# Moving the Strassen products of one half ahead of its plain output products, in an attention kernel fused with a ReGLU feed-forward

## The chip, the cores and the metric

The kernel runs on one core of one Trainium2 chip. The metric is the device time of one execution in microseconds (us). TensorE (PE) does the matmuls and loads their weights (PEld); VectorE (DVE), ScalarE (ACT) and GpSimd (POOL) work element by element; DMAs are issued from the queues of SyncE (SP), POOL and ACT. Each engine works through its own instructions in program order.

## The reference

Attention over 4 batches, 8 heads, 768 positions and 64 dimensions, with a mask (8 global positions and the last 96) and a distance bias per head; its output, 3072 tokens x 512, goes through a gated feed-forward layer with 1536 hidden columns.

```python
scores = scale * np.matmul(q, k.transpose(0, 1, 3, 2))
...
scores = scores + bias[None, :, :, :]
scores = np.where(keep, scores, -1000000000.0)
...
a = np.exp(scores)
a = a / (np.sum(a, axis=-1, keepdims=True) + 1e-09)
return np.matmul(a, v).astype(np.float32)
...
x = np.ascontiguousarray(attn_out.transpose(0, 2, 1, 3)).reshape(B * S, H * D)
gate = np.maximum(x @ w_gate, 0.0)
val = x @ w_val
return (gate * val @ w_out).astype(np.float32)
```

## The kernel before

**Halves.** The work is cut into 8 halves: half s is batch s // 2 and 384 of its positions. In the text "half 2" is s = 2, the third one (the diff's title counts from one: its "second half" is s = 1 and its "third half" s = 2). Attention runs one half ahead of the feed-forward layer, so while the feed-forward work of one half fills TensorE, the next half's attention is placed between.

**Attention of a half** (`attention_pieces`) goes by four pairs of heads, p = 0 to 3. `piece_qk` issues the scores of a pair (L397, 8 matmuls in an even half, 10 in an odd one) into four banks of the PSUM pool `x`, then ScalarE's exps (L406, tile `es`) and VectorE's masks (L359). `piece_av` (the P·V product, L427) takes one bank of `x` for each head; ScalarE takes the logarithm of the row sums (L436, `lnd`) and, after the second head, the exp that gives the inverse (L441, `rcp`). `piece_norm` (L446, "norm p") multiplies on VectorE into chunk p of `xT`, the feed-forward input, one multiply for each head; each frees one bank of `x`. The pool `x` has five banks, used in turn: an allocation waits for the release of the one five allocations earlier.

**Keys and queries of a half** (`early_pieces`) come through ks and qs (DMA), eight casts on GpSimd (L363, into `kqc`), three DMA transposes on SyncE's queue (L368, into `kqT`), and four reorderings (`piece_order`, "order p", L259 to L265, three copies on GpSimd each) into `kT`, the keys in the order that the scores read.

**Feed-forward of a half** (`ffn_pieces(c)`) has two lists. f1: for each of 12 column groups fc a `gate` product (4 matmuls, L518; ScalarE's relu L525) and a `val` product (4 matmuls, L518; VectorE multiplies into `ht`, L531). f2: the output product, of three tiles of 128 tokens. A *plain* tile is 12 matmuls of 512 columns in four parts of three (L538), a copy by ScalarE (L543, tile `osb`) and a store on SyncE's queue (L544). From the second half on, tiles 0 and 1 are instead computed by seven Strassen-like products `p4 p3 p1 p2 p5 p6 p7`, six matmuls of 256 columns each (L581):

- p4, p3 and p1 go to banks of the pool `ff` named d, c and a, and ScalarE copies them into two `osb` tiles (L597, L601, L605).
- p2 and p5 each take one bank of the pool `x`, and VectorE adds and subtracts them (L609, L610; L614, L615).
- p6 goes on adding to bank c; VectorE adds it (L622) and the tile is stored from SyncE's queue (L623). p7 does the same with bank a (L627, L628). Both stores run through `store` (L591).

The products read sums of `ht` (`sum_de`, `sum_cb`, `sum_ad`, L574, L565, L569) and five sums of wo, computed once in ten steps on VectorE (`wo_sum`, L804, tiles `bs`). The pool `ff` has three banks, used in turn, the `osb` pool three buffers, used in turn.

The next half begins with `begin` (L546): gate and value matmuls of column group 0 over the first three chunks of `xT` (6 matmuls); the fourth chunk's matmuls come behind the first scores of the half after it.

**The order** on every engine is the order in which `weave` (L659) calls the pieces. It walks through a list of feed-forward pieces with given weights (mostly 0.65, sums 0), and after each it issues those placed items whose position, as a share of the list's total, has been reached. `spread` (L654) gives a list of items evenly spaced positions between two shares.

**The stage of the change** (L821) runs the last four column groups of half 0 and half 1, then f2 of half 0 (three plain tiles, 12 parts) and f2 of half 1 (one plain tile with two sums between, then the products). Its total weight is 25.35. Into it are placed two reorderings of half 2 on ScalarE, the attention of half 2, the early pieces of half 3 and the ten `wo_sum` steps. The stages behind it (L827) each hold one half's f1 and f2, the attention of the next half, and the early pieces of the one after.

Of the kernel before, what the change touches and what calls it, by code (L numbers as in the profile page):

```python
# [15 lines left out]
def kernel(  # L16
# [124 lines left out]
    def fill_ones(eng, i, j):  # L141
        eng.memset(vbuf[i][:, j, :].bitcast(mybir.dt.uint32).rearrange(
            "p (h z) -> p h z", z=D // 2)[:, 0 : 2 * H + 1 : 2, :], 0x3F803F80)
# [217 lines left out]
    def piece_cast(s, p, i):  # L361
        of = (ks_of, qs_of)[i]
        nc.gpsimd.tensor_copy(  # L363
            kqc[:, :, i].rearrange("t n (h d) -> t h n d", d=D)[:, 2 * p : 2 * p + 2],
            of[s][:, 2 * p : 2 * p + 2, :].rearrange("t e (n d) -> t e n d", n=NN))

    def piece_x(s, n):
        nc.sync.dma_start_transpose(  # L368
            out=kqT[s % 2].rearrange("d i p t -> d (i p) t")[:, :, n * 128 : (n + 1) * 128],
            in_=kqc[:, n].rearrange("t i z -> t (i z)"))  # L370

    def piece_order(s, p):
        b, half = divmod(s, 2)
        copy = nc.scalar.copy if s == 2 and p >= 2 else nc.gpsimd.tensor_copy
        put_keys(copy, copy, kT[b % 2][p], kNb[s % 2][:, p], half)

    def early_pieces(s):
        out = [(0.0, lambda p=p, i=i: piece_cast(s, p, i)) for i in range(2) for p in range(HP)]
        out += [(0.0, lambda n=n: piece_x(s, n)) for n in range(NN)]
        out += [(0.0, lambda p=p: piece_order(s, p)) for p in range(HP)]  # L380
        return out
# [26 lines left out]
    def piece_qk(s, p, g):  # L408
        if g == 0:
            pair_scores(s, p)  # L410
        if g < 2:
            pair_exps(s, p, g)
        if g > 0:
            masks(s, p, g - 1, steps_later)

    def piece_av(s, p, e):
        b, half = divmod(s, 2)
        h = 2 * p + e
        vb = vbuf[b % 2]
        av = psum["x"].tile([128, 512], FP32, name="x_ps")  # L420
        av_of[s, p, e] = av
        av3 = av[:, 0:QH].rearrange("d (n p) -> d n p", n=NN)
        todo = [by[half, j] for g in steps_later[half] for j in g]
        for i, (j, a, w, m) in enumerate(todo):
            es, c = es_of[s, p, j]
            z0 = 2 * D * h + (D if e == 0 else 0)
            nc.tensor.matmul(av3[:, :, a : a + w],  # L427
                             lhsT=vb[:, j, z0 : z0 + 128],
                             rhs=es[:, e, c : c + NN * w].rearrange("k (n p) -> k n p", n=NN),
                             start=(i == 0), stop=(i == len(todo) - 1),  # L430
                             skip_group_check=True)
        o0, d0 = (0, 64) if e == 0 else (64, 0)
        if e == 0:
            av_of[s, p, "l"] = rc_pool.tile([128, QH], FP32, name="lnd")
        ln = av_of[s, p, "l"]
        nc.scalar.activation(ln[o0 : o0 + 64], av[d0 : d0 + 64, 0:QH], AF.Ln, bias=0.0, scale=1.0)  # L436
        if e == 1:
            if s not in xT_of:
                xT_of[s] = xt_pool.tile([128, N_DC, QH], BF16, name="xT")
            rc = av_of[s, p, "r"] = rc_pool.tile([128, QH], FP32, name="rcp")  # L440
            nc.scalar.activation(rc, ln, AF.Exp, bias=0.0, scale=-1.0)  # L441

    def piece_norm(s, p):
        for e in range(2):
            r = slice(64 * e, 64 * e + 64)
            nc.vector.tensor_tensor(xT_of[s][r, p, :], av_of[s, p, e][r, 0:QH], av_of[s, p, "r"][r],  # L446
                                    op=ALU.mult)
# [45 lines left out]
    def attention_pieces(s):  # L493
        QK = lambda p: [(0.15, lambda g=g: piece_qk(s, p, g)) for g in range(3)]
        AV = lambda p: [(0.29, lambda e=e: piece_av(s, p, e)) for e in range(2)]
        N = lambda p: [(0.0, lambda: piece_norm(s, p))]
        g = QK(3)
        a = AV(2)
        gap = [(0.0, lambda: None)]
        return (QK(0) + QK(1) + AV(0) + N(0) + gap + QK(2) + AV(1) + N(1) + gap  # L500
                + g[0:1] + a[0:1] + g[1:2] + a[1:2] + g[2:3] + N(2) + AV(3) + N(3))
# [152 lines left out]
    def spread(items, first, last):  # L654

        n = len(items)
        return [(first + (i + 0.5) / n * (last - first), f) for i, (_, f) in enumerate(items)]

    def weave(f_items, *placed):  # L659
        total = sum(t for t, _ in f_items)  # L660
        a_items = sorted((x for p in placed for x in p), key=lambda x: x[0])
        done, ai = 0.0, 0
        for t, f in f_items:
            f()
            done += t
            while ai < len(a_items) and a_items[ai][0] * total <= done:
                a_items[ai][1]()
                ai += 1
        for _, f in a_items[ai:]:
            f()  # L670
# [84 lines left out]
    f1_0, f2_0 = ffn_pieces(0)  # L755
    f1_1, f2_1 = ffn_pieces(1)
# [20 lines left out]
    for f in ("m1 g0 m3 v0 m2 g1 K3 K2 m0 g3 K1 S30 S31 g2 K0 S20 v3 S11 v1 S21 A3 N3 v2 S00 S01 "  # L777
              "g5 A2 S10 g4 g6 A0 N2 v5 v4 N0 A1 N1 g7 v7 v6").split():
        i = int(f[1])
# [20 lines left out]
    def wo_sum(name, part):  # L800
        i = slice(part * N_FC // 4, (part + 1) * N_FC // 4)
        x, y = (wo_sb[:, (int(b[1]) - 1) * N_FC // 2 :][:, i, (int(b[2]) - 1) * DM // 2 : int(b[2]) * DM // 2]
                for b in (name[:3], name[4:]))
        nc.vector.tensor_tensor(late["bs"][name][:, i], x, y, op=ALU.add if "+" in name else ALU.subtract)  # L804

    G = [slice(2 * GW * i, 2 * GW * (i + 1)) for i in range(N_FC // GW)]
# [7 lines left out]
    for f in (*casts[:7], lambda: nc.gpsimd.tensor_copy(held, wo_sb[0:1, N_FC - 1, 0:1]),  # L814
# [3 lines left out]
    load_v_half(3)  # L818
    weave(f1_1[G[0]])
    weave(f1_1[G[1]], [(0.1 + 0.12 * j, lambda j=j: fill_ones(nc.vector, 0, j)) for j in range(NT)])  # L820
    weave(f1_0[G[2]] + f1_1[G[2]] + f2_0 + f2_1,  # L821
          [(0.33, order_k[2]), (0.38, order_k[3])],
          spread(attention_pieces(2), 0.375, 0.9), spread(early_pieces(3), 0.58, 0.88),
          spread([(0.0, lambda name=name, part=part: wo_sum(name, part)) for name in late["bs"] for part in range(2)],
                 0.1, 0.74))

    for c in range(2, NHALF):  # L827
        placed = []
# [6 lines left out]
        f1, f2 = ffn_pieces(c)  # L835
# [36 lines left out]
```

## Time and profile before

| | us |
|---|---|
| median of 3 runs (lowest, highest) | 242.32 (241.63, 242.71) |
| profiled execution | 242.01 |
| its span, first to last instruction | 240.2 |
| f1 of half 1 ends, f2 of half 0 begins | about 57 |
| first plain part of half 1 | 67.5 |
| first product | 71.4 |
| first gate matmul of half 2 | 76.6 |
| first scores of half 3 | 78.8 |

The granted TensorE clock is 1.000 over the span. Times in the profile are us from the first instruction. A timeline line gives start, length, engine, line, operation, output and inputs, and a count of merged instructions; behind it, in brackets, the engine's idle time before and what ended it. PE's matmuls overlap: a matmul's duration is longer than the step to the next one's start, so where PE's pace matters, the text goes by starts.

### The profile page before, as it was taken

How to read it: one execution, taken by the hardware profiler on the slowest of the kernel's cores; microseconds unless marked ns; L12 is line 12 of the kernel's file. 1: busy time of each engine (PE TensorE's matmuls, PEld its weight loads, DVE VectorE, ACT ScalarE, POOL GpSimd, SP SyncE). 2: the span in 40 equal slices, each digit the busy share in tenths (PEclk: the TensorE clock that was granted, in tenths of full speed). 3: DMA queues.
4: the chain of work that ended last, by engine and by line, in shares of the span. 5: the costliest groups of instructions: out<-in, count | busy, mean ns of one | idle time of the engine just before them, and what ended most of it. 6: DMA issues, size and time to landing. Idle time of an engine off the chain costs nothing.

```text
span 240.2 us, 5363 instructions
## 1 busy us (share of the span) xinstructions
PE 233.5 (97%) x1945; PEld 146.3 (61%) x1945; DVE 172.5 (72%) x456; ACT 153.6 (64%) x347; POOL 87.0 (36%) x202
## 2 busy tenths in 40 slices
PE   7999999999998999999999999999999999999994
PEld 3655556665457566676568566676658566676663
DVE  6785965769587597866888679766887677764643
ACT  5897873438775777738774777738874677733330
POOL 6767892308414733541539042721414000000000
PEclk9999999999999999999999999999999999999999
DMA  6999999994975995299245966198241200030003
GB/s 197 186 197 178 257 231 220 184 161 80 268 162 128 235 213 97 44 143 289 54 91 71 246 181 114 20 179 265 50 88 44 90 0 0 3 128 4 4 26 105
DMA packets 69603, 31.42 MB, mean 131 GB/s; under 512 B 47160, under 2 KB 66616, under 8 KB 69576
## 3 DMA queue, kind: packets, MB, share of 16 engines
q0 software_dynamic: 31744, 8.71, 35.1%
q1 hardware_dynamic: 36616, 21.45, 34.3%
q10 hardware_dynamic: 1216, 0.92, 1.2%
q8 instruction: 15, 0.25, 0.4%
q14 instruction: 12, 0.10, 0.1%
HBM read 28.41 MB, written 6.29 MB: 144 GB/s over the span
## 4 chain that ended last, share of the span: by engine, by line
PE 91%; ACT 3%; DVE 2%; DMA 1%; issue 1%; ACTq 0%; DVEq 0%
PE ff_ps L518 54%; PE ff_ps L538 9%; PE ff_ps L581 8%; PE x_ps L427 5%; PE x_ps L397 4%; PE x_ps L581 3%; PE t_ps L459 2%; PE s_ps L341 2%; DMA kq<-in_k_dram 1%; PE t_ps L272 1%; ACT lnd L436 1%; PE t_ps L310 1%; DVE xT L446 1%; ACT rcp L441 1%; PE s_ps L321 1%
## 5 line engine op out<-in xcount | busy, mean ns | idle before, releaser
L518 PE MATMUL ff_ps<-xT,wv 128*128 128x384 bf16 x384 | 80.2, 326 | 1.1 <-DVE osb L622 1.0
L518 PE MATMUL ff_ps<-xT,wg 128*128 128x384 bf16 x384 | 80.6, 326 | 0.4 <-ACT grelu L525 0.4
L531 DVE TENSOR_TENSOR ht<-ff_ps,grelu 128x384 bf16<-128x384 f32 x96 | 53.1, 554 | 29.2 <-PE ff_ps L518 16.7
L525 ACT ACTIVATE grelu<-ff_ps 128x384 bf16<-128x384 f32 x96 | 47.3, 492 | 35.9 <-DVE ht L531 17.8
L518 PEld LDWEIGHTS <-wv 128*128 128x128 bf16 x384 | 36.1, 97 | 24.1 <-issue 2.3
L518 PEld LDWEIGHTS <-wg 128*128 128x128 bf16 x384 | 35.9, 98 | 24.1 <-issue 0.9
L406 ACT ACTIVATE es<-x_ps 128x360 bf16<-128x360 f32 (+2 forms) x96 | 36.7, 443 | 20.8 <-PE x_ps L397 20.7
L359 DVE TENSOR_TENSOR es<-es,m_all 128x432 bf16<-128x432 bf16 (+4 forms) x108 | 31.0, 333 | 8.5 <-ACT es L406 8.1
L446 DVE TENSOR_TENSOR xT<-x_ps,rcp 64x384 bf16<-64x384 f32 x48 | 26.6, 555 | 9.7 <-ACT rcp L441 9.0
L436 ACT ACTIVATE lnd<-x_ps 64x384 f32<-64x384 f32 x48 | 23.3, 485 | 12.3 <-PE x_ps L427 11.6
L538 PE MATMUL ff_ps<-wo_sb,ht 128*128 128x512 bf16 x120 | 30.2, 379 | 0.0
L363 POOL CAST kqc<-ks 128x384 bf16<-128x384 f32 x24 | 11.4, 518 | 30.7 <-DMA ks<-in_k_dram 30.5
L137 POOL DMA_DIRECT2D vbuf<-in_v_dram x25 | 21.6, 876 | 2.3 <-DMA wv<-in_moe_w_val_dram 1.8
L427 PE MATMUL x_ps<-es,vbuf 128*128 128x216 bf16 (+4 forms) x216 | 21.5, 225 | 0.0
L427 PEld LDWEIGHTS <-vbuf 128*128 128x128 bf16 x216 | 15.8, 97 | 7.7
L538 PEld LDWEIGHTS <-ht 128*128 128x128 bf16 x120 | 10.8, 97 | 9.4
L363 POOL CAST kqc<-qs 128x384 bf16<-128x384 f32 x24 | 12.2, 548 | 11.9 <-DMA qs<-in_q_dram 11.9
L263 POOL COPY kT<-kqT 128x240 bf16<-128x240 bf16 x16 | 7.1, 441 | 24.5 <-DMA kqT<-kqc 22.4
L441 ACT ACTIVATE rcp<-lnd 128x384 f32<-128x384 f32 x24 | 12.6, 524 | 0.8
L259 POOL COPY kT<-kqT 128x360 bf16<-128x360 bf16 x10 | 5.7, 572 | 19.3 <-DMA kqT<-kqc 19.3
L347 ACT ACTIVATE ef<-s_ps 128x720 bf16<-128x720 f32 (+2 forms) x16 | 11.0, 711 | 1.7 <-PE s_ps L341 1.3
L397 PE MATMUL x_ps<-kqT,kT 64*128 64x216 bf16 (+4 forms) x216 | 11.6, 224 | 0.2
(115 smaller groups left out, 252.1 us busy)
## 6 DMA issues: line engine op xcount, KB each, us to landing
out_dram<-osb SPq DMA_DIRECT2D x22, 256.0 KB, 3.6
ks<-in_k_dram SPq DMA_DIRECT2D x6, 768.0 KB, 7.0
qs<-in_q_dram SPq DMA_DIRECT2D x6, 768.0 KB, 13.9
vbuf<-in_v_dram POOLq DMA_DIRECT2D x21, 120.0 KB, 8.1
wg<-in_moe_w_gate_dram POOLq DMA_DIRECT2D x3, 512.0 KB, 8.8
wv<-in_moe_w_val_dram POOLq DMA_DIRECT2D x3, 512.0 KB, 10.0
wo_sb<-in_moe_w_out_dram POOLq DMA_DIRECT2D x1, 1536.0 KB, 20.3
kq<-in_q_dram ACTq DMA_DIRECT2D x2, 192.0 KB, 4.4
```

The costliest lines, as they stand in the source:

```text
L137: nc.gpsimd.dma_start(out=v_dst(b, NG + r0, NG + r0 + n, j), in_=v[b, :, KT * j + r0 : KT * j + r0 + n, :].rearrange("h p d -> p h d"))
L359: nc.vector.tensor_mul(for_all, for_all, mk)
L363: nc.gpsimd.tensor_copy(kqc[:, :, i].rearrange("t n (h d) -> t h n d", d=D)[:, 2 * p : 2 * p + 2], of[s][:, 2 * p : 2 * p + 2, :].rearrang ...
L406: nc.scalar.activation(es[:, e, 0:c], banks[e][:, 0:c], AF.Exp, bias=0.0, scale=scale)
L427: nc.tensor.matmul(av3[:, :, a : a + w], lhsT=vb[:, j, z0 : z0 + 128], rhs=es[:, e, c : c + NN * w].rearrange("k (n p) -> k n p", n=NN), s ...
L436: nc.scalar.activation(ln[o0 : o0 + 64], av[d0 : d0 + 64, 0:QH], AF.Ln, bias=0.0, scale=1.0)
L446: nc.vector.tensor_tensor(xT_of[s][r, p, :], av_of[s, p, e][r, 0:QH], av_of[s, p, "r"][r], op=ALU.mult)
L518: nc.tensor.matmul(st[key][:, 0:QH], lhsT=w_of(w, dc, fc), rhs=xT_of[c][:, dc, :], start=(dc == 0), stop=(dc == N_DC - 1))
L525: nc.scalar.activation(gr, psg[:, 0:QH], AF.Relu, bias=0.0, scale=1.0)
L531: nc.vector.tensor_tensor(ht[:, fc, :], psv[:, 0:QH], st["gr", fc], op=ALU.mult)
L538: nc.tensor.matmul(ps2, lhsT=ht[:, fc, n * 128 : (n + 1) * 128], rhs=wo_sb[:, fc, :], start=(fc == 0), stop=(fc == N_FC - 1))
L581: nc.tensor.matmul(st[key][:, 0:D2], lhsT=left(i), rhs=right(i), start=start and i == 0, stop=stop and i == N2 - 1, skip_group_check=not s ...
```

## The change

In the stage at L821 the list of f2 pieces is put together in another order. Half 0's tiles 0 and 1 come first as before; the sums `sum_ad(3, 6)` and `sum_cb(3, 6)` move into half 0's tile 1; then come half 1's products, p4 to p7 with `sum_de(9, 12)` behind p4; then half 1's plain tile, then half 0's tile 2. The total weight stays 25.35. The attention of half 2 is spread up to 0.93 of the stage instead of 0.9, the steps of `wo_sum` up to 0.6 instead of 0.74. The placed early pieces of half 3 keep their shares. No instruction is added or removed.

```diff
-    weave(f1_0[G[2]] + f1_1[G[2]] + f2_0 + f2_1,
+
+    plain, sum_1, sum_2, products = [f2_1[i] for i in (0, 1, 3, 5)], f2_1[2], f2_1[4], f2_1[6:]
+    f2 = f2_0[:6] + [sum_1] + f2_0[6:7] + [sum_2] + f2_0[7:8] + products + plain + f2_0[8:]
+    weave(f1_0[G[2]] + f1_1[G[2]] + f2,
           [(0.33, order_k[2]), (0.38, order_k[3])],
-          spread(attention_pieces(2), 0.375, 0.9), spread(early_pieces(3), 0.58, 0.88),
+          spread(attention_pieces(2), 0.375, 0.93), spread(early_pieces(3), 0.58, 0.88),
           spread([(0.0, lambda name=name, part=part: wo_sum(name, part)) for name in late["bs"] for part in range(2)],
-                 0.1, 0.74))
+                 0.1, 0.6))
```

The order of the placed items against the pieces of f2, from p4 on in the changed list: after p4 the second exps of pair 2; after p3 its last masks and the first P·V of pair 1; after p1 the second one; after p2 norm 1; after p6 the scores of pair 3 and the first transpose of half 3; after p7 a P·V of pair 2 and the other two transposes. The stores of p6 and p7 are issued with p6 and p7. In the list before, all three transposes were issued among half 1's plain parts, ahead of the products.

## The prediction

> **What bounds the kernel now.** I read the page first: busy shares and the chain that ended last.
>
> ```profile
> span 240.2 us, 5363 instructions
> PE 233.5 (97%) x1945; PEld 146.3 (61%) x1945; DVE 172.5 (72%) x456; ACT 153.6 (64%) x347; POOL 87.0 (36%) x202
> PE 91%; ACT 3%; DVE 2%; DMA 1%; issue 1%; ACTq 0%; DVEq 0%
> ```
>
> TensorE is 91% of the chain, and the change issues the same 1945 matmuls, so only places where PE stands still can move the time. Next, PE's timeline from 56 to 80 us, the stage that the change rearranges:
>
> ```profile
> 58.67 0.45 PE L397 MATMUL x_ps<-kqT,kT 64*128 64x216 bf16 x8
> ...
> 62.94 0.80 PE L397 MATMUL x_ps<-kqT,kT 64*128 64x216 bf16 x8
> ...
> 68.21 0.79 PE L397 MATMUL x_ps<-kqT,kT 64*128 64x216 bf16 x8
> ...
> 76.56 0.49 PE L518 MATMUL ff_ps<-xT,wg 128*128 128x384 bf16 x2
> 78.06 0.48 PE L518 MATMUL ff_ps<-xT,wv 128*128 128x384 bf16 x2 [1.01 <-DVE osb L622]
> ...
> 78.80 0.48 PE L397 MATMUL x_ps<-kqT,kT 64*128 64x216 bf16 x10
> ```
>
> Eight score matmuls need 0.45, twice they take 0.80: 0.35 lost each time. Two gate matmuls at 76.56 need 0.33 (0.163 each) and the next starts at 78.06: 1.17 lost. In all 1.87 us, so without waits the first scores of half 3, at 78.80, would start at 76.93. That is my measuring point: behind it the program's order on every engine is unchanged. Then VectorE's, SyncE's and GpSimd's timelines, for who holds the banks and who feeds those scores:
>
> ```profile
> 58.10 0.48 DVE L359 TENSOR_TENSOR es<-es,m_all 128x432 bf16<-128x432 bf16 x2
> 65.88 1.24 DVE L359 TENSOR_TENSOR es<-es,m_all 128x432 bf16<-128x432 bf16 x2 [0.94 <-ACT es L406]
> 68.09 1.14 DVE L446 TENSOR_TENSOR xT<-x_ps,rcp 64x384 bf16<-64x384 f32 x2 [0.50 <-ACT rcp L441]
> 77.59 0.41 DVE L622 TENSOR_TENSOR osb<-ff_ps,osb 128x256 f32<-128x256 f32 x1
> ```
> ```profile
> 68.55 0.33 SPq L544 DMA_DIRECT2D out_dram<-osb  x1
> 69.00 4.13 SPq L368 DMA_TRANSPOSE kqT<-kqc  x3
> 78.03 0.81 SPq L591 DMA_DIRECT2D out_dram<-osb  x2
> ```
> ```profile
> 64.95 2.00 POOL L363 CAST kqc<-qs 128x384 bf16<-128x384 f32 x4 [1.07 <-DMA qs<-in_q_dram]
> 75.15 0.42 POOL L263 COPY kT<-kqT 128x240 bf16<-128x240 bf16 x1 [8.19 <-DMA kqT<-kqc]
> 179.00 0.42 POOL L263 COPY kT<-kqT 128x240 bf16<-128x240 bf16 x1 [7.70 <-DMA kqT<-kqc]
> ```
>
> The addition of L622 ends at 78.00 and lets go of the ff bank that PE waited for. The three transposes start at 69.00, 70.33 and 71.83; the first reordering copy runs 3.32 after the third, at 75.15, the three copies of a pair take 0.8, so half 3's first keys lie ready at 75.95, 2.85 before they are read. The copies then idle, as does SyncE between 73.8 and 78.03.
>
> **The sums of wo, sooner.** The same 10 at 0.55 (0.47 from start to start). I take nothing for it. VectorE is busy for 4.20 of 6.50 us in 44.0 to 50.5 and for 5.64 of 6.50 in 50.5 to 57.0, and the sums run there behind a gate product that VectorE has no part in; without that cover a sum delays the next ht multiply by 0.47. The last sum goes from 69.26 to about 64.5.
>
> **The products, ahead of eight plain parts.** Widths of PE pieces by starts: plain part 0.647, product 0.655, one P·V 0.274, scores of a pair 0.474. Nothing changes up to 61.0; then P·V of pair 0 at 61.01 and 61.28, plain parts to 63.50, scores of pair 2 to 63.97, p4 and p3 to 65.28, P·V and p1 to 66.21, P·V to 66.48, p2, p5, p6 to 68.45, scores of pair 3 to 68.92, p7, eight plain parts and four P·V to 75.85, the begin matmuls (6 at 0.163) to 76.83: 76.93 again for the scores of half 3, if nothing waits.
>
> *The 1.17 goes.* Of three ff banks in turn, the gate's now follows p1's (L627, about 71) and the value's follows the plain product copied at about 74. Were they late, 1.17 would come back.
>
> *The first 0.35 goes, the second grows.* The x pool has five banks; the sixth matmul of pair 2's scores waits for norm 0's first half, due at 63.61 (its P·V ends at 61.55; 0.2 to ScalarE, 0.49, 0.52, 0.56 by the rows at 61.75 to 63.38, and 0.23 of queue); it comes at 63.72, so no wait. But p2 and p5 now take two x banks ahead of pair 3's scores, whose third bank thus waits for norm 1's second half. When is that? ScalarE: p1's copy (L605) writes the osb buffer that the first store leaves, issued at 61.17 and landing 5.9 us later in this trace, at 67.09. Then L605 0.27, log 0.52, exp 0.56, two norms 2 x 0.59: 69.6. That matmul was due at 68.67: 0.96 lost.
>
> VectorE's queue ahead of norm 1 is sum_cb, masks, sum_de, masks, L609, L610. Three of these meet the four q casts of 64.95 to 66.95, and the row at 65.88 shows what that means: 0.71 for the 128x432 mask that takes 0.38 at 58.10. With 0.30 turned into 0.63 (a factor 2.1) sum_cb, a pair's masks and sum_de end at 67.15, the next masks at 67.75, L610 at 68.4, just as the exp is ready: free by this row. The Trainium skill, SBUF — State Buffer, section "Who interferes with whom", says that a two-input VectorE operation and a GpSimd one that reads SBUF shut each other out for a whole instruction. By an estimate from that page's rule and the cast's 0.50, three operations would each wait 0.5, and the stores below would come some 0.4 later than I take.
>
> *A new wait: the transposes.* On SyncE's queue, p6's store (L623) now stands ahead of the first transpose and p7's (L628) ahead of the second; before, both stood behind. SyncE waits in order, so the transposes, their reordering copies, GpSimd's next loads of v behind these, and half 3's first scores all wait for L622. Call its end E. After norm 1 come L614, L615 and L622: E = 69.6 + 0.33 + 0.33 + 0.42 = 70.7. First transpose at E + 0.47 (wake and store), third at E + 3.7 (2.83 between first and third, 0.42 for the store in between), first copy at E + 7.05, keys at E + 7.85, scores at E + 7.9 = 78.6. PE is there at 76.93 + 0.96 = 77.89: 0.73 lost.
>
> **Sum.** 1.87 lost before, 0.96 + 0.73 = 1.69 after: 0.2 us gained. The profiled execution took 242.01 (span 240.2, 1.8 around it), hence 241.8; it lies 0.3 under the median of the three runs, 242.32, so on that scale 242.1. Everything hangs on E: the gain is 70.9 − E.
>
> Bounds. E: with no queue at all on ScalarE behind that P·V's end at 66.48, E is 69.97 (+0.9); if the casts come half a microsecond later and stretch the last masks too, from 0.60 to the 1.24 of the row at 65.88, norm 1 starts 0.6 later and E is 71.3 (−0.4). The transposes, from the third's start to the first copy: 3.32 here; in the four later stages (third starts at 94.65, 120.33, 148.15 and 174.16, copies at 98.70, 124.09, 151.39 and 179.00) 4.05, 3.76, 3.24 and 4.84. I take 3.32: the same three transfers at the same place, also right behind a 256 KB store. The others give −0.7 to +0.3. GpSimd's v loads start some 2.5 us later than 78.13; they serve the stage after next, and landed at 91.8: no cost. The attention's later end lets norm 3 finish at about 77.2, and its chunk is read behind the scores at 78.6: 1.4 of cover, beyond which it would cost what it is late.
>
> **Rivals.**
> A, the transposes hide. Then only the wait at pair 3's scores is left: 0.35 as now instead of 0.96 makes 1.52 gained, 240.8. For: the 2.85 us of slack that the keys have now. Against: this needs E at 69.0, and even an empty ScalarE queue gives 69.97; or transposes over a microsecond quicker than any row.
> B, slower: the transposes, split by p7's store, land as late as at 174 to 179 us. Its place is SyncE's queue at 70.7 to 75; its price 4.84 − 3.32 = 1.5 over the forecast, so 1.3 lost: 243.6. It decides from 3.5 on for a loss at all, and from 4.7 on for a loss of 1.2. For: three of five rows lie above 3.5, and now two stores share that queue with the transposes. Against: half a microsecond of queue would not do it, and the store between them should have landed (2.3 after the one at 68.55) before the third's data move.
> C, the change does nothing where it counts: VectorE frees the bank sooner but the new waits eat all of it. That is my forecast within 0.2 and shares its chance.
>
> **How the numbers follow.** Forecast with C, 0.66: 242.1, its own range 241.3 (E 69.97, 3.24) to 243.4 (E 71.3, 4.05). A 0.16, B 0.18. The range runs from 241.0, close to A, to 243.6, where B stands, so that about one in five is left out. A measurement of this kernel can tell about 0.5% (1.2 us) from no change: the runs of before spread over 0.45%. A lies beyond it below, B above, the forecast's own range within: 0.16, 0.66, 0.18.
>
> **What would show it.** Right: the gate and value matmuls of half 2 run on without a gap; the last wait of this stage is that of half 3's first scores, for GpSimd's copies; the three transposes start near 71.2 instead of 69.0, behind a store; pair 3's scores are stretched to about 1.4 us. Wrong: transposes still near 69 (the order on SyncE is misread), a gap before the begin matmuls, or waits beyond 100 us that were not there. E itself is read off as the end of L622's first instance.

## The result, and the profile after

The changed kernel is slower: 245.06 us median of 6 runs (243.54 to 246.70) against 242.63 of the kernel before (6 runs, 241.63 to 242.82), a ratio of 1.0105 with a 95% interval of 1.0061 to 1.0150. The forecast was 242.1, in a range up to 243.6. The runs also lie further apart than those of before. The profiled execution took 244.21, span 242.4, which is 2.2 us over the profiled one of before; with the others up to 246.70, it shows one of the milder losses. In all ratios of this document, runs more than 1.5% over their kernel's fastest are left out: 6 of 12 in the run with late loads and 1 of 6 in the order-only one, the profiled execution among them in both.

First the page: TensorE's share of the last chain has fallen from 91% to 87%. (A few records are missing from this trace, hence 5352 instructions against 5363; the program issues the same ones.)

```profile
span 242.4 us, 5352 instructions
PE 87%; DMA 4%; ACT 3%; DVE 3%; issue 2%; POOL 0%; SPq 0%; POOLq 0%; ACTq 0%
```

PE's timeline of the stage and of the stage behind it, for the lines shown of before:

```profile
63.54 0.45 PE L397 MATMUL x_ps<-kqT,kT 64*128 64x216 bf16 x8
...
68.50 0.28 PE L397 MATMUL x_ps<-kqT,kT 64*128 64x216 bf16 x4
69.30 0.25 PE L397 MATMUL x_ps<-kqT,kT 64*128 64x216 bf16 x1 [0.52 <-DVE xT L446]
69.90 0.33 PE L397 MATMUL x_ps<-kqT,kT 64*128 64x216 bf16 x3 [0.35 <-DVE xT L446]
70.16 0.83 PE L581 MATMUL ff_ps<-bs,de 128*128 128x256 bf16 x6
...
77.42 0.49 PE L518 MATMUL ff_ps<-xT,wv 128*128 128x384 bf16 x2
...
78.45 0.74 PE L397 MATMUL x_ps<-kqT,kT 64*128 64x216 bf16 x10 [0.21 <-POOL kT L263]
...
87.87 0.81 PE L518 MATMUL ff_ps<-xT,wg 128*128 128x384 bf16 x4 [1.74 <-DVE ht L531]
```

Up to 79 us this is the forecast. The scores of pair 2 no longer wait, those of pair 3 last until 70.16 (1.28 us lost), the begin matmuls run on, and half 3's first scores wait for GpSimd's copies and are stretched (0.28 + 0.27). They end at 79.12, where they ended at 79.21 before: 0.1 gained. The last line is new: from 85.96, where the next gate product was due, to 87.87 TensorE waits for a multiply of VectorE, 1.91 us. Before, it ran on there without a wait:

```profile
85.41 0.81 PE L518 MATMUL ff_ps<-xT,wv 128*128 128x384 bf16 x4
86.06 0.81 PE L518 MATMUL ff_ps<-xT,wg 128*128 128x384 bf16 x4
```

Behind it the offset to before is 1.8 us at half 4's first scores and stays within 0.4 of that to the end.

SyncE's, VectorE's and GpSimd's timelines say how the two places hang together:

```profile
70.99 0.33 SPq L591 DMA_DIRECT2D out_dram<-osb  x1
71.43 1.30 SPq L368 DMA_TRANSPOSE kqT<-kqc  x1
72.82 0.53 SPq L591 DMA_DIRECT2D out_dram<-osb  x1
73.41 2.70 SPq L368 DMA_TRANSPOSE kqT<-kqc  x2
```
```profile
70.54 0.42 DVE L622 TENSOR_TENSOR osb<-ff_ps,osb 128x256 f32<-128x256 f32 x1
...
83.89 3.46 DVE L359 TENSOR_TENSOR es<-es,m_all 128x432 bf16<-128x432 bf16 x5
87.27 1.01 DVE L531 TENSOR_TENSOR ht<-ff_ps,grelu 128x384 bf16<-128x384 f32 x2
```
```profile
77.97 0.42 POOL L263 COPY kT<-kqT 128x240 bf16<-128x240 bf16 x1 [9.59 <-DMA kqT<-kqc]
...
81.50 3.62 POOL L137 DMA_DIRECT2D vbuf<-in_v_dram  x4
85.10 2.06 POOL L363 CAST kqc<-ks 128x384 bf16<-128x384 f32 x4
87.11 1.95 POOL L363 CAST kqc<-qs 128x384 bf16<-128x384 f32 x4
```

The first transpose starts at 71.43 instead of 69.00, behind p6's store; the reorderings of half 3 start at 77.97 instead of 75.15; so GpSimd issues the loads of v for half 4 until 85.1 instead of 82.3. The k of half 4 landed at 83.49, while those loads were still being issued; the q landed at 85.96 (89.72 before). The earlier q goes with the later loads in every trace: with loads of v as late as here or later it landed at 85.96 to 87.42 (five runs), with loads at about the time of before or earlier at 89.23 to 90.36 (five runs). So k and q casts run in one block from 85.10 to 89.06, and five masks of half 3 take from 83.89 to 87.27 on VectorE. Before, it was this:

```profile
83.98 1.46 DVE L359 TENSOR_TENSOR es<-es,m_all 128x432 bf16<-128x432 bf16 x5
```
```profile
78.69 3.61 POOL L137 DMA_DIRECT2D vbuf<-in_v_dram  x4
84.66 2.06 POOL L363 CAST kqc<-ks 128x384 bf16<-128x384 f32 x4 [2.35 <-DMA ks<-in_k_dram]
89.84 2.09 POOL L363 CAST kqc<-qs 128x384 bf16<-128x384 f32 x4 [3.12 <-DMA qs<-in_q_dram]
```

The multiply of `ht` behind the masks comes 1.9 us later, and its ff bank is the one that the next gate product waits for.

### The profile page after: what moved, and what is told of

Same layout as the page of the kernel before. It is cut to its first block, busy times and chain, and to the rows that moved or that the text cites. A ratio compares the mean times of both kernels' runs of the same rounds, so it can differ in the third digit from the quotient of the medians.

```text
span 242.4 us, 5352 instructions
## 1 busy us (share of the span) xinstructions
PE 233.1 (96%) x1937; PEld 146.0 (60%) x1945; DVE 175.4 (72%) x456; ACT 153.8 (63%) x347; POOL 87.0 (36%) x202
## 4 chain that ended last, share of the span: by engine, by line
PE 87%; DMA 4%; ACT 3%; DVE 3%; issue 2%; POOL 0%; SPq 0%; POOLq 0%; ACTq 0%
PE ff_ps L518 52%; PE ff_ps L581 8%; PE ff_ps L538 7%; PE x_ps L427 5%; PE x_ps L397 4%; PE x_ps L581 3%; DMA out_dram<-osb 2%; PE t_ps L459 2%; DMA kqT<-kqc 1%; PE s_ps L341 1%; PE t_ps L677 1%; PE t_ps L310 1%; PE t_ps L272 1%; DVE es L359 1%; ACT ef L347 1%
## 5 line engine op out<-in xcount | busy, mean ns | idle before, releaser
L359 DVE TENSOR_TENSOR es<-es,m_all 128x432 bf16<-128x432 bf16 (+4 forms) x108 | 33.4, 356 | 8.0 <-ACT es L406 7.6
L538 PE MATMUL ff_ps<-wo_sb,ht 128*128 128x512 bf16 x112 | 29.1, 379 | 0.4
```

The lines of the kernel that those rows point to most:

```text
L359: nc.vector.tensor_mul(for_all, for_all, mk)
L538: nc.tensor.matmul(ps2, lhsT=ht[:, fc, n * 128 : (n + 1) * 128], rhs=wo_sb[:, fc, :], start=(fc == 0), stop=(fc == N_FC - 1))
```

## The experiments

**Theory 1:** the stores ahead of the transposes on SyncE's queue start a chain (late transposes, late reorderings, late loads of v) whose end is a collision of GpSimd's casts with VectorE's masks in the next stage. **Theory 2:** the new order itself overloads VectorE there. **Theory 3:** the cause is the spacing, not the order. Ratios below are to the kernel before, with 95% intervals. Code is cut at "...". Line numbers of some of these kernels are shifted by a few.

**The stores behind the transposes (e1).**

```diff
-            store(1, slice(0, DM) if c < NHALF - 1 else c1, nc.sync if c < NHALF - 1 else nc.scalar)
+            if c == 1:
+                late["behind"] = [lambda: store(1, slice(0, DM))]
...
+    def last_x(f=E3[10][1]):
+        f()
+        for g in late["behind"]:
+            g()
+
+    E3[10] = (0.0, last_x)
```

The store of p7 is put off in the same way; `E3[10]` is the third transpose of half 3.

> The changed kernel with one thing put back: the stores of half 1's products p6 and p7 are issued on SyncE's queue behind the three transposes of half 3 instead of ahead of them. Theory 1 (the held transposes start the chain: late reorderings, late loads of v, k and q casts of half 4 back to back on GpSimd, which then slow a run of masks of half 3): the transposes start right behind the q casts, near 68.5 us instead of 71.4, the waits at 78.45 and 78.83 (0.28 and 0.27 us) and the one at 87.87 (1.91 us) are gone, 2.46 us in all: 241.8 on the scale of the profiled 244.21, a ratio to before of about 0.998, and the runs lie as close together as those of before. Theory 2 (the new order of products and attention alone overloads VectorE in the next stage): the 1.91 stays, only 0.55 go: ratio about 1.008.

Measured: 0.9976 (0.9959 to 0.9994), median 241.75. The profiled execution took 241.72.

```profile
67.32 4.06 SPq L368 DMA_TRANSPOSE kqT<-kqc  x3
71.48 1.03 SPq L591 DMA_DIRECT2D out_dram<-osb  x2
```
```profile
83.38 1.15 DVE L359 TENSOR_TENSOR es<-es,m_all 128x432 bf16<-128x432 bf16 x5
```

The transposes start even before 69, the five masks take 1.15, and TensorE waits neither at 78 nor at 88. Putting two DMA issues back is worth 1.3% against the changed kernel (by the two ratios) and turns the loss into a small gain. The new order and its load on VectorE are still there, so theory 2 falls.

**The casts held back (e2).** Everything of the changed kernel stays late; only the casts of half 4 wait.

```diff
+        if c == 2:
+            placed.append([(5.3 / 22.75, lambda: nc.gpsimd.tensor_copy(held2, late["ht"][0:1, 3, 0:1]))])
```

> The changed kernel with GpSimd's casts of half 4 held back: a one-element copy on GpSimd, ahead of them, reads the product of column group 3 of half 2, which VectorE writes behind the masks that were slow (83.9 to 87.3 us). The transposes stay late. Theory 1: these masks take about 1.4 us instead of 3.4, the wait at 87.87 us (1.91) is gone, the waits of 0.28 and 0.27 at 78.5 stay: about 242.3 on the scale of the profiled 244.21, ratio to before near 1.001; casts that come later may cost some tenths elsewhere. Theory 2 (masks slow or late without the casts having a part in it): the wait stays, ratio about 1.010.

Measured: 1.0013 (0.9998 to 1.0027), median 242.63. GpSimd, then VectorE:

```profile
81.62 3.61 POOL L137 DMA_DIRECT2D vbuf<-in_v_dram  x4
85.68 0.18 POOL L842 COPY held<-ht 1x1 bf16<-1x1 bf16 x1 [0.44 <-DVE ht L532]
85.80 1.84 POOL L363 CAST kqc<-ks 128x384 bf16<-128x384 f32 x4
```
```profile
83.99 1.15 DVE L359 TENSOR_TENSOR es<-es,m_all 128x432 bf16<-128x432 bf16 x5
```

The same loads are issued during the same masks, and the masks run at full pace: issuing loads alone does not slow them, and without casts due the slowing is gone. The wait at 87.87 is gone. What is left is the stage that the prediction had summed up, 0.3 us slower than before by this ratio where 0.2 faster was forecast.

**The order alone, and the spacing alone (e3, e4).**

```diff
 e3, against the changed kernel
-          spread(attention_pieces(2), 0.375, 0.93), ...
+          spread(attention_pieces(2), 0.375, 0.9), ...
...
-                 0.1, 0.6))
+                 0.1, 0.74))
 e4, against the kernel before
-          spread(attention_pieces(2), 0.375, 0.9), ...
+          spread(attention_pieces(2), 0.375, 0.93), ...
...
-                 0.1, 0.74))
+                 0.1, 0.6))
```

> Only the new order of the products and plain parts; attention up to 0.9 and sums of wo up to 0.74 as before. Theory 1: the stores still stand ahead of the transposes, so the loss is there as in the changed kernel, ratio about 1.01, with a wait of 1 to 3 us near 88 us. Theory 3 (the loss comes from the later attention or the earlier sums): ratio at or under 1.000.

> Only the two spacings (attention up to 0.93, sums of wo up to 0.6) in the order of before. Theory 1: the transposes stay where they were, nothing is lost: ratio 0.998 to 1.003. Theory 3: ratio about 1.01.

Measured: the order alone 1.0121 (1.0088 to 1.0154), the spacing alone 0.9982 (0.9971 to 0.9993). The whole loss belongs to the order, and theory 3 falls. With the order alone the wait in the next stage was 3.2 us in the profiled execution, the longest of its six (248.51). The spacing alone is a small gain: both 0.35 waits are gone, and the wait at the begin matmuls has grown from 1.17 to 1.42.

**Loads behind the casts (e5).** Are casts that run enough, or do loads ahead of them add to it?

```diff
-            load_v_half(c + 2)
+            if c != 2:
+                load_v_half(c + 2)
...
+        if c == 2:
+            def v_loads():
+                load_v_globals(2)
+                for j in range(4):
+                    load_v(2, j)
+
+            placed.append([(0.51, v_loads), (0.61, lambda: spread_v_globals(2))])
```

> The changed kernel with GpSimd's five loads of v for half 4 issued behind the eight casts of half 4 instead of ahead of them. The transposes stay late, and the casts run against the masks of half 3 as soon as k lands (83.5 us). Theory 1a (a cast that runs slows the masks, nothing else does): the five masks at about 83.9 take some 2.4 us, as a mask under a cast took 0.63 to 0.71 instead of 0.30 to 0.38; of the 1.91 us on TensorE about 1 stays: ratio 1.004 to 1.006. Theory 1b (worse is a cast that is ready and stands behind the loads of v on GpSimd, since in the changed kernel the masks are slow from 83.9 on, and the first cast is shown at 85.1 only): without loads ahead the masks take under 2 us and the wait near 88 us is under 0.5: ratio 0.999 to 1.003.

Measured: 1.0033 (1.0015 to 1.0052). The casts start as k lands, at 83.66.

```profile
83.69 0.69 DVE L574 TENSOR_TENSOR de<-ht 128x384 bf16<-128x384 bf16 x1
84.30 2.06 DVE L359 TENSOR_TENSOR es<-es,m_all 128x432 bf16<-128x432 bf16 x5
```

`sum_de` takes 0.69 instead of 0.36, the masks 2.06, and TensorE waits 0.85 instead of 1.91. The masks and the wait speak for theory 1a: running casts alone cost nearly half of it. The ratio does not decide, its interval overlaps the bands of both. Loads alone cost nothing (the run with held casts), so the other 1.06 us came only where loads were under way and casts due behind them. But here the casts also start 1.4 us earlier than in the changed kernel and pause at 85.79 for q, and the last two masks run at full pace in that pause; how much of the 1.06 lies in this timing and how much in the loads ahead is not shown.

**Late loads in the kernel before (e6).** Neither the new order nor the spacing, only the end of the chain.

```diff
-            load_v_half(c + 2)
+            if c != 2:
+                load_v_half(c + 2)
...
+        if c == 2:
+            def late_v():
+                nc.gpsimd.tensor_copy(held2, late["ht"][0:1, 0, 0:1])
+                load_v_half(4)
+
+            placed.append([(1.35 / 22.75, late_v)])
```

> The kernel before, with GpSimd's loads of v for half 4 held by a one-element copy that reads the first product of half 2, so that they are issued from about 81 to 85 us instead of 78.1 to 82.3, as in the changed kernel. The stage's order and the transposes are those of before. Theory 1 (late loads of v, with k of half 4 landing while they are issued, slow the masks of half 3): the masks at 84 us take 2.5 us or more instead of 1.4, and TensorE waits 1 to 3 us near 88: ratio 1.004 to 1.010. Theory 2 (the order of the changed stage is needed for it): ratio 0.999 to 1.002.

Measured: 1.0055 (1.0022 to 1.0088); the median of all 12 runs is 246.41, from 242.47 to 248.07. VectorE, GpSimd and PE in the profiled execution (247.12):

```profile
84.09 4.94 DVE L359 TENSOR_TENSOR es<-es,m_all 128x432 bf16<-128x432 bf16 x5
```
```profile
81.90 3.60 POOL L137 DMA_DIRECT2D vbuf<-in_v_dram  x4
85.50 1.99 POOL L363 CAST kqc<-ks 128x384 bf16<-128x384 f32 x4
87.44 1.95 POOL L363 CAST kqc<-qs 128x384 bf16<-128x384 f32 x4
```
```profile
89.55 0.65 PE L519 MATMUL ff_ps<-xT,wg 128*128 128x384 bf16 x3 [3.22 <-DVE ht L532]
```

The collision is made in the old order, with the old transposes, by one late issue of loads. Theory 1's last link stands without the rest of the change. The 4.94 us and the wait of 3.4 us (by starts) are those of this one execution; no other of this kernel was traced.

**Towards a better version (e7, e8).** Both start from the run with the stores behind the transposes; `A2[17]` is the scores of pair 3.

```diff
 e7
+    A2 = spread(attention_pieces(2), 0.375, 0.93)
+    A2[17] = (19.51 / 25.35, A2[17][1])
 e8, also
-    late["osb"] = ctx.enter_context(tc.tile_pool(name="osb", bufs=3, reuse_waits="tile"))
+    late["osb"] = ctx.enter_context(tc.tile_pool(name="osb", bufs=4, reuse_waits="tile"))
```

> The kernel with the two stores behind the transposes, and the scores of pair 3 issued behind p7 instead of ahead of it. In that kernel TensorE waits 0.25, 0.38 and 0.59 us among these scores, for banks that norm 1 frees. p7 needs 0.66 us on TensorE and none of these banks: if the banks are the cause, it takes about 0.65 of these 1.2 away, 241.1 against a before of 242.4, ratio 0.995. If something else is late (VectorE's queue behind norm 1), the wait moves to the next allocations and the ratio stays near 0.9975.

> As the run with the scores behind p7, and the osb pool has four buffers instead of three, so that ScalarE's copy of p1 (L605) need not wait for the first store to land (0.56 us in the changed kernel), and the logarithm, exp and norm 1 behind it come earlier. If that wait sets norm 1, the rest of the wait at pair 3's scores shrinks by 0.3 to 0.5 us: ratio 0.993 to 0.994. If VectorE's queue sets norm 1, nothing changes against that run.

Measured: e7 0.9977 (0.9960 to 0.9994), median 241.79; e8 0.9960 (0.9942 to 0.9979), median 241.33, the lowest median here and 1.4% under the changed one by the two ratios; the intervals of e1, e7 and e8 overlap. PE in e7, then in e8:

```profile
69.31 0.38 PE L397 MATMUL x_ps<-kqT,kT 64*128 64x216 bf16 x5
69.93 0.33 PE L397 MATMUL x_ps<-kqT,kT 64*128 64x216 bf16 x3 [0.24 <-DVE xT L446]
70.71 0.43 PE L427 MATMUL x_ps<-es,vbuf 128*128 128x216 bf16 x4 [0.45 <-DVE osb L615]
```
```profile
69.40 0.53 PE L397 MATMUL x_ps<-kqT,kT 64*128 64x216 bf16 x8
70.38 0.43 PE L427 MATMUL x_ps<-es,vbuf 128*128 128x216 bf16 x4 [0.45 <-DVE osb L615]
```

With the scores behind p7, the next allocation of the x pool, P·V, waits for L615, which frees p5's bank. From the start of p6 to this P·V, TensorE loses 1.2 us in e1, 1.0 in e7 and 0.6 in e8 (starts, less the widths that the prediction gives). So e7 took away 0.2 where 0.65 was expected, since most of the wait came back one allocation later, and as a whole it cannot be told from e1. The fourth osb buffer took away another 0.4, as expected of that step: norm 1 starts at 68.73 in e7, right behind the exp that waited for L605, and at 68.41 in e8, right behind L610, where VectorE's queue sets it. The expected ratios (0.995, then 0.993 to 0.994) were missed by what e7 fell short.

## Why the prediction was wrong

**The sum of the stage was right.** E, the end of L622, was put at 70.7 and came at 70.96; the first transpose was due at 71.2 and came at 71.43; half 3's first scores were due at 78.6 and came at 78.45. The 1.17 and the first 0.35 went as said. The wait for the store's landing ahead of L605 is there (0.56 us). Two terms were mis-sized: the second 0.35 grew to 1.28, not 0.96, because norm 1 began at 68.70 and not at 68.44, and the wait of half 3's first scores was 0.55, not 0.73. Together 1.83 us of waits, for 1.69 predicted. All four signs that the prediction named for being right came true (the scores of pair 3 took 1.66, longer than the 1.4 named), and none of those for being wrong: the loss lay at 86 to 88 us, where it had named no sign. The casts' slowing of VectorE in this stage showed too (the masks at 66.36 took 1.21), and cost nothing on norm 1, as worked out.

**The step that failed** is in the bounds: "GpSimd's v loads start some 2.5 us later than 78.13; they serve the stage after next, and landed at 91.8: no cost." They did start 2.8 us later, and their data were indeed in time (89.2). But the loads were only followed to their own reader. What stands behind them on GpSimd's queue, the casts of half 4, and what is DMAed beside them, the q of half 4, were not. In place of the zero, the masks of half 3 took 3.46 us instead of 1.46, and TensorE waited 1.91 us in the profiled execution. The run with held casts shows that without that part the forecast holds to about half a microsecond (1.0013, and 242.33 profiled for 241.8); the run with late loads in the kernel before shows that this part alone makes a loss of the same kind (1.0055).

**The evidence was in the prediction itself.** It quoted a mask under casts at twice its time, and used it for the q casts of half 3 only. In the trace of before, the k casts of half 4 start at 84.66, while the five masks of 83.98 run until 85.44, and the last of them already takes 0.63 instead of 0.33: the two just touch. A shift of 2.8 us in GpSimd's queue ought to have been followed up to there. The measuring point, behind which "the program's order on every engine is unchanged", was the wrong premise: the order was unchanged, the meeting of two engines was not.

**The rivals.** A did not come about, for the reason given: E was far from 69.0. (By the prediction's own formula, 1.52 gained needs E at 70.9 − 1.52 = 69.4, not 69.0; 70.96 is far from both.) B named the right queue but the wrong price: the third transpose started at 74.76 and the first copy 3.21 later, which is as quick as the quickest row of before (3.24). Its sign was right, and its mechanism was not the one that decided.

**The rule weighed against the row.** The Trainium skill, SBUF — State Buffer, section "Who interferes with whom", was cited for whole-instruction exclusion between a two-input VectorE operation and GpSimd's reads, and was priced there at one cast (0.5 us) for each operation. The runs agree with an exclusion and not with that price: a mask can be held for much longer than one cast. In the changed kernel's profiled execution a 128x96 mask took 1.20 us (84.94 to 86.14), which takes 0.20 undisturbed. In the profiled execution of the kernel before with late loads, one mask, which takes 0.33 undisturbed, took 2.43 beside six casts:

```profile
86.60 2.43 DVE L359 TENSOR_TENSOR es<-es,m_all 128x336 bf16<-128x336 bf16 x1
```
```profile
86.39 1.09 POOL L363 CAST kqc<-ks 128x384 bf16<-128x384 f32 x2
87.44 1.95 POOL L363 CAST kqc<-qs 128x384 bf16<-128x384 f32 x4
```

The casts run without a gap from 85.50 to 89.39, and the mask ends at 89.03, after four of them have begun and ended beside it.

## What to carry to other kernels

When a change delays a DMA issue on an in-order queue, follow that delay through every later instruction on each queue that it touches, until some slack has swallowed it, and look at what then runs at the same time on engines that share something; a cost of nothing that rests on a transfer's own deadline covers the transfer alone. Before stores are moved, ask what stands behind them on the issuing queue: here two stores of finished results, ahead of three transposes that could start earlier, cost 1.3%. If a trace shows an operation at twice its time beside another engine, list all places where the two nearly meet.

## What the runs showed of the hardware

- **Casts on GpSimd and two-input multiplies on VectorE.** The same five masks took 1.15 us with no cast near (also while loads of v were issued), 1.46 with casts from their last mask on, 2.06 under casts alone, 3.46 and 4.94 where k had landed while GpSimd still issued loads ahead of the casts. In the changed kernel the masks are slow from 83.89 on (0.68 for the first, which takes 0.38 otherwise), although the first cast is shown at 85.10. Why a cast that stands behind loads slows VectorE already was not settled; spans on GpSimd are rough.
- **TensorE's clock after a long wait.** After waits of over 3 us the granted clock fell for some us. The order-only run's stretches after its 3.2 us wait show it (length; PE, PEld, DVE, ACT and POOL busy; then PEclk, DMA share, GB/s):

```profile
87.00:90.80 3.80, 0.79 (x6) 0.37 (x5) 3.80 (x5) 1.36 (x3) 3.67 (x8) 1.00 1.79 120
90.80:95.60 4.80, 4.78 (x27) 2.34 (x27) 3.02 (x8) 2.41 (x6) 0.00 (x0) 0.64 0.84 153
95.60:100.00 4.40, 4.40 (x35) 2.77 (x33) 2.87 (x7) 2.88 (x7) 3.37 (x12) 1.00 0.08 16
```

  At 0.64 for 4.8 us, that is an estimated 1.7 us of lost work on top of the wait (4.8 x 0.36). The kernel before with late loads shows 0.62 over 4.5 us after its 3.4 us wait. After the 1.91 us of the changed kernel's profiled execution the clock stayed at 1.00. The Trainium skill, TensorE: Matmul & The Clock Gate, section "Part 1: The HAM clock gate", gives about 3.4 us of idling as what turns the clock down. The runs come near that: 1.9 us was too short, 3.2 and 3.4 were enough, though 3.2 is a little under the page's figure, and no trace has a wait between 1.9 and 3.2. The run of 246.70 of the changed kernel has a mean clock of 0.993, its other five 0.998 or more. In the kernel before with late loads the six runs above 247 us have 0.984 to 0.993, the six below 246 have 0.999 or 1.000. So a collision that is long enough costs nearly two microseconds more at once, which fits the spread of these runs.
